# Sigmoid attention into a token and channel mixer: the first loads by other queues, weights in full-width rows, and batch 0's second channel product moved into the 64x64 runs of batch 2

## The chip, the cores and the metric

One core of one Trainium2 chip. The number is device time in microseconds (us) of one execution, the median of three runs. The engines named here are PE (matmuls; PEld is its weight load), DVE (VectorE), ACT (ScalarE), POOL (GpSimd, which here issues the loads that cast fp32 to fp16) and SP (which issues transposing DMAs and stores). Each has its own list of instructions, in the order in which the kernel issues them, and waits for the others through semaphores.

## The reference

For 8 batches, 12 heads, 448 positions and head width 64:

```python
scores = scale * np.matmul(q, k.transpose(0, 1, 3, 2)) - np.log(S)
attn = 1.0 / (1.0 + np.exp(-scores))
out = np.matmul(attn, v)
...
x = attn_out.transpose(0, 2, 1, 3).reshape(B, S, H * D)      # 8 x 448 x 768
xt = x.transpose(0, 2, 1)
h = np.maximum(xt @ w_tok1, 0.0) @ w_tok2                    # 448 -> 256 -> 448
u = x + h.transpose(0, 2, 1)
h2 = np.maximum(u @ w_ch1, 0.0) @ w_ch2                      # 768 -> 1536 -> 768
return u + h2
```

## The kernel before, in words

**Units.** The 12 heads of a batch are taken as three units of four heads: unit u holds heads 2u and 2u+1 in partitions 0 to 63 and heads 6+2u and 7+2u in partitions 64 to 127. There are 24 cycles, c = 3b + u; c5 is batch 1, unit 2, and c6, c7, c8 are batch 2. The program is written in one order by hand (a manual schedule), and each engine keeps that order.

**What a cycle holds.** `qk` (line 173) makes seven score blocks, four 64x64 matmuls each, and ACT turns each into `att` by one sigmoid. `av` (198) multiplies by v, for the unit before, and DVE casts the result from two PSUM banks into `xT` (217), then copies its last 64 columns (221). `xtrans_dma` (231) has SP transpose `xT` into `xn`. `tok_tail` and `tok1` (257, 275) are the first token product, `ytrans` (302) the second, whose sum with `xT` DVE writes to `ut` (314). A batch's three units done, `ch1` (332) makes the first channel product (12 blocks of six 128x128 matmuls, DVE's relu at 350 into `h2`), and `ch2`, `ch2_pair`, `ch2_last` (397, 443, 476) the second, which is stored from tile `outs`.

**Two forms of the second channel product.** `ch2` makes a group (128 rows, half the 768 columns) with twelve 128x128 matmuls. `ch2_pair` makes both halves at once: eight of the twelve row blocks as `quads` (354), four 64x64 matmuls each, which stand between the 64x64 matmuls of `qk` and `av`, and the other four as 128x128 matmuls in `rest`. The tensor u is added either by DVE, from `un` (a transposing DMA of `ut`, `utrans`, 319), or, for batch 0, by PE: three matmuls with the identity (416).

**Order of the cycles.** Batch 0 and c3 to c5 are written out (662 to 795). c6 to c8 are a loop of their own (798 to 847) in which `pending` deals out pieces: batch 0's `ch2` and `ch2_last` in c6 and c7, batch 1's `ch1` in c8. c5 holds the first two `ch2` groups of batch 0. From c9 (`ONE_RUN`) each cycle is the same: two score blocks, the first turn of `ch2_pair` of batch b-2, a block, `av`, two blocks, the second turn, a block, `tok_tail`, the last block, `tok1`, `rest`, `ytrans`; the third cycle of a batch also holds `ch2_last` and the next batch's 12 `ch1` blocks.

**PSUM.** Four banks (m0 to m3) are dealt in turn, in the opening by the string `OPENING_BANKS`; two tiles of two banks hold scores. From c9 on the pair uses m2 and m3, and `av`, `tok_tail` and `ytrans` use m0 and m1.

**Transposed q and k.** From batch 2, unit 1 on they come by DMA: DVE regroups a unit (`relayout`, 114, into `rel`), SP transposes (`dma_transpose`, 132, into `tr`). `by_unit` (147) lists the eight pieces for the last two units of batch 2, `through_dma` (138) those for a whole batch; the list `copies` is popped between PE's pieces. POOL holds back the loads of the batch after by a small copy that reads the end of `tr` (`gated_loads`, 723, line 725; and 793): the gate runs when that transpose has landed. `raw` has one buffer each for k and q, so batch 3's k and q can be loaded only when batch 2's have been regrouped.

**The loads.** All of v, most of q and k, and the weights go by POOL's queue in the order in which they stand (531 to 600, then 783). Each such load holds one of eight semaphores and waits for the one eight before it. `c1` and `c2` come in two column halves each. The first unit's q comes as fp32 by the ACT and SP queues (525) into `first_q`, cast by DVE and ACT (639, 640).

Of the kernel before, what the change touches and what calls it, by code (L numbers as in the profile page):

```python
# [9 lines left out]
FP16 = mybir.dt.float16  # L10
# [13 lines left out]
OPENING_BANKS = "20130130130130213021302130213021313021213021302130202130123102302132132032"  # L24
# [3 lines left out]
def kernel(  # L28
# [41 lines left out]
    first_q = pc.tile([128, 2, NJ, E], FP32, name="first_q")  # L70
# [326 lines left out]
    def ch2(b, t, half, n0=0, n1=NCB):  # L397
# [6 lines left out]
        for cb in range(n0, n1):  # L404
            nc.tensor.matmul(  # L405
                out=ps[:, 0:DH],
                lhsT=h2[b][:, cb, 128 * t : 128 * t + 128],
                rhs=c2[:, cb, cols],
                start=(cb == 0),
                stop=(cb == NCB - 1 and b in un),  # L410
            )
        if n1 < NCB:
            return
        if b not in un:
            for n in range(NU):
                nc.tensor.matmul(
                    out=ps[:, 128 * n : 128 * n + 128],
                    lhsT=uts[b % 2][:, NU * half + n, 128 * t : 128 * t + 128],
                    rhs=ident[:, :],
                    start=False,  # L420
                    stop=(n == NU - 1),
                )
        ch2_out(b, t, half, ps)

# [18 lines left out]
    def ch2_pair(b, t):  # L443
# [17 lines left out]
        def rest():  # L461
            for p in range(2):
                for n in range(n_quads, NCB):
# [5 lines left out]
                        stop=(n == NCB - 1),  # L469
                    )  # L470
                ch2_out(b, t, p, ps[p])
# [52 lines left out]

    for g, queue in enumerate((nc.scalar, nc.sync)):
        queue.dma_start(
            out=first_q[64 * g : 64 * g + 64].rearrange("p hi j e -> p hi (j e)"),
            in_=q[0, 6 * g : 6 * g + 2].rearrange("h (p j) e -> p h (j e)", j=NJ),
        )

    def load_first_k(j0, j1):
        for g in range(2):
            nc.gpsimd.dma_start(
                out=raw_tile(0, "k")[64 * g : 64 * g + 64, 0, :, j0:j1, :].rearrange(
                    "p hi j e -> p hi (j e)"
                ),
                in_=k[0, 6 * g : 6 * g + 2].rearrange("h (p j) e -> p h (j e)", j=NJ)[
                    :, :, j0 * E : j1 * E
                ],
            )  # L540

    load_first_k(0, 2)
# [7 lines left out]
    load_first_k(2, NJ)  # L550
# [21 lines left out]
    def load_c1(half):  # L572
        cols = slice(CC // 2 * half, CC // 2 * half + CC // 2)
        nc.gpsimd.dma_start(
            out=c1[:, :, cols],
            in_=moe_w_ch1.rearrange("(db d) c -> d db c", db=NDB)[:, :, cols],
        )

    def load_c2(half):
        cols = slice(DH * half, DH * half + DH)  # L580
        nc.gpsimd.dma_start(
            out=c2[:, :, cols],
            in_=moe_w_ch2.rearrange("(cb c) d -> c cb d", cb=NCB)[:, :, cols],
        )
# [3 lines left out]
    load_c1(0)  # L588
# [3 lines left out]
    load_c1(1)  # L592
# [4 lines left out]
    load(2, "k", k, 1, NU)  # L597
    load(2, "q", q, 1, NU)
    load_c2(1)
    load(2, "v", v, 0, 1)  # L600

# [22 lines left out]
    def keep_warm(n):  # L624
# [12 lines left out]
    keep_warm(16)  # L637

    nc.vector.tensor_copy(out=raw_tile(0, "q")[:, 0, :, 0:4, :], in_=first_q[:, :, 0:4, :])
    nc.scalar.activation(  # L640
        out=raw_tile(0, "q")[:, 0, :, 4:NJ, :], in_=first_q[:, :, 4:NJ, :], func=COPYF
    )
    pe_transpose(0, "q", 0, 0, 4)
    pe_transpose(0, "q", 0, 4, NJ, on_scalar=True)
    pe_transpose(0, "k", 0, 0, 2)
    keep_warm(3)
# [12 lines left out]
    def tok(u):  # L659
# [6 lines left out]
            [tp(0, 0, "k", 2), lambda: keep_warm(3)],  # L666
# [44 lines left out]
    ch1(0, 0, 0, 4)  # L711
    qk(1, 0, 4)
    qk(1, 0, 5)
    ch1(0, 1, 0, 4)
# [21 lines left out]
    ONE_RUN = 3 * NU  # L736
    LATER = 0

    by_half = sorted(((t, half) for t in range(3) for half in range(2)), key=lambda g: g[1])
    for c, cb in ((N_FIRST, 3), (N_FIRST + 1, 8)):  # L740
# [31 lines left out]
        if u == 2:  # L772
            copies = by_unit(2, 1)
        whole(cb + 2)
        if c - 1 not in ON_DMA:
            xtrans(*before)
        for t in ("k", "q"):
            pe_transpose(ahead[0], t, ahead[1])
        whole(cb + 3)
        if c == N_FIRST:  # L780
            tok1(*before)
# [3 lines left out]
        else:  # L785
            for w, f in pieces_ch2(0, by_half[:2]):
                f()
                if copies:
                    copies.pop(0)()
            while copies:  # L790
                copies.pop(0)()

            nc.gpsimd.tensor_copy(out=gate[:, :], in_=tr[2, "q"][:, 1, NJ - 1, 126:128])
            load(2, "v", v, 1, NU)
            gated_loads(b)

    pending, copies = [], []
    for c in range(2 * NU, ONE_RUN):
        b, u = divmod(c, NU)
        before, ahead = divmod(c - 1, NU), divmod(c - 2, NU)  # L800


        if c in (2 * NU, 2 * NU + 2):
            first = c
            if c == 2 * NU:
                pending, shares = [*pieces_ch2(0, by_half[2:]), *pieces_last(0)], [15, 15]
            else:
                pending, shares = list(pieces_ch1(1)), [30]
            total = sum(w for w, f in pending)
            spent = 0  # L810

        def work(share):
            goal = 3 * sum(shares[: c - first]) + share * shares[c - first]
            done = 0
# [146 lines left out]
```

## Time and profile before

| | |
|---|---|
| median of 3 runs | 360.21 us (360.18 to 361.25) |
| the profiled execution | 360.48 us |
| its span, first to last instruction | 358.7 us |
| PE busy | 351.7 us, 4099 matmuls |
| DVE, ACT, POOL busy | 184.7, 169.5, 56.3 us |
| DMA, mean over the span | 145 GB/s, 52.11 MB |
| first sigmoid of ACT starts at | 8.54 us |
| start of c5, c6, c7, c8, c9 (first `qk` matmul) | 50.66, 63.74, 73.81, 84.31, 102.95 us |

Times inside the profile are us from the span's start. A line of the timeline gives start, duration, engine, source line, operation, output and inputs, count, and in brackets how long the engine had been idle before and what released it. In the list of DMA issues the last number is the time from issue to landing. A matmul's duration is longer than its distance to the next one (matmuls overlap in the array), so PE's time is read from starts.

### The profile page before, as it was taken

The numbers are of one execution on the slowest core, as the hardware profiler recorded it, in microseconds if no ns is written. First come the engines' busy times: TensorE is split into PE (matmuls) and PEld (weight loads), VectorE is DVE, ScalarE is ACT, GpSimd is POOL, SyncE is SP. The second block draws the span as 40 slices with busy tenths as digits, with TensorE's granted clock in tenths as the row PEclk, the third lists the DMA queues.
The fourth block names the chain that finished last, engine by engine and source line by source line (L and its number), as shares of the span: only waits on it lengthen the run. The fifth ranks groups of instructions, "written<-read, shape, count | busy, mean of one in ns | idle before, by whom it ended". The sixth has DMA issues, their size and how long they took to land.

```text
span 358.7 us, 9225 instructions
## 1 busy us (share of the span) xinstructions
PE 351.7 (98%) x4099; PEld 204.3 (57%) x4099; DVE 184.7 (51%) x343; ACT 169.5 (47%) x215; POOL 56.3 (16%) x98
## 2 busy tenths in 40 slices
PE   7999999999999999999999999999999999999995
PEld 4555565555456655666556655666456655555553
DVE  2376558247455555454645655455553445516521
ACT  3996844675458810787038820777028830010000
POOL 8974330220120004000040004000010000000000
PEclk9999999999999999999999999999999999999999
DMA  7999999999998797959989597949963680047014
GB/s 122 175 176 198 205 204 196 164 203 234 186 176 153 115 199 133 206 96 195 186 125 185 121 202 128 207 94 149 227 88 75 104 155 0 13 106 141 14 46 110
DMA packets 104375, 52.11 MB, mean 145 GB/s; under 512 B 76432, under 2 KB 101264, under 8 KB 104336
## 3 DMA queue, kind: packets, MB, share of 16 engines
q1 hardware_dynamic: 78944, 29.70, 46.0%
q0 software_dynamic: 25168, 21.50, 39.0%
q8 instruction: 32, 0.52, 0.6%
q10 hardware_dynamic: 224, 0.33, 0.4%
q14 instruction: 7, 0.06, 0.0%
HBM read 43.45 MB, written 11.01 MB: 152 GB/s over the span
## 4 chain that ended last, share of the span: by engine, by line
PE 92%; ACT 4%; DMA 1%; DVE 1%; issue 0%; DVEq 0%; ACTq 0%
PE c L339 30%; PE c L362 12%; PE c L405 10%; PE qk L181 10%; PE xa L208 8%; PE tk L286 6%; PE c L464 5%; PE yt L307 5%; PE c L488 5%; ACT att L188 4%; DMA first_q<-in_q_dram 1%; PE tp_k L161 1%; PE tp_q L161 1%; PE tk L267 1%; PE heat L626 0%; DVE ut L314 0%
## 5 line engine op out<-in xcount | busy, mean ns | idle before, releaser
L188 ACT ACTIVATE att<-qk,att_bias 128x896 f16<-128x896 f32 x168 | 154.7, 1016 | 114.3 <-PE qk L181 114.2
L339 PE MATMUL c<-ut,c 128*128 128x448 f16 x552 | 108.2, 353 | 0.0
L339 PEld LDWEIGHTS <-c 128*128 128x128 f16 x552 | 52.5, 98 | 52.3 <-issue 3.5
L350 DVE TENSOR_SCALAR h<-c 128x448 f16<-128x448 f32 x96 | 59.5, 624 | 43.6 <-PE c L339 42.0
L181 PE MATMUL qk<-tr_q,tr_k 64*64 64x448 f16 x672 | 57.9, 359 | 0.2
L428 DVE TENSOR_TENSOR o<-un,c 128x384 f32<-128x384 f16 x42 | 23.3, 554 | 49.7 <-PE c L464 28.1
L217 DVE CAST xT<-xa 128x448 f16<-128x448 f32 x48 | 27.7, 620 | 40.3 <-PE xa L208 40.3
L362 PE MATMUL c<-c,h 64*64 64x384 f16 x960 | 46.6, 323 | 0.0
L208 PE MATMUL xa<-att,raw_v 64*64 64x448 f16 x672 | 39.6, 349 | 0.0
L405 PE MATMUL c<-c,h 128*128 128x384 f16 x216 | 37.5, 326 | 0.0
L362 PEld LDWEIGHTS <-h 64*64 64x64 f16 x960 | 28.1, 107 | 11.8
L181 PEld LDWEIGHTS <-tr_k 64*64 64x64 f16 x672 | 21.2, 105 | 20.1 <-issue 12.3
L300 ACT ACTIVATE h<-tk 128x256 f16<-128x256 f32 x42 | 14.4, 417 | 33.4 <-PE tk L286 33.4
L405 PEld LDWEIGHTS <-h 128*128 128x128 f16 x216 | 20.5, 98 | 14.4 <-issue 1.4
L314 DVE TENSOR_TENSOR ut<-xT,yt 128x448 f16<-128x448 f16 x48 | 27.4, 614 | 2.6 <-PE yt L307 2.5
L725 POOL COPY gate<-tr_q 128x2 f16<-128x2 f16 x6 | 1.1, 184 | 170.4 <-DMA tr_q<-rel_q 170.4
L208 PEld LDWEIGHTS <-raw_v 64*64 64x64 f16 x672 | 20.4, 107 | 11.0 <-issue 0.7
L464 PE MATMUL c<-c,h 128*128 128x384 f16 x120 | 22.0, 326 | 0.0
L307 PE MATMUL yt<-w,h 128*128 128x448 f16 x96 | 21.9, 353 | 0.0
L286 PE MATMUL tk<-xn,w 128*128 128x256 f16 (+1 forms) x156 | 21.8, 274 | 0.1
L286 PEld LDWEIGHTS <-w 128*128 128x128 f16 (+1 forms) x156 | 13.4, 98 | 7.4 <-issue 5.2
L488 PE MATMUL c<-c,h 128*64 128x384 f16 x192 | 17.3, 328 | 0.0
(58 smaller groups left out, 195.0 us busy)
## 6 DMA issues: line engine op xcount, KB each, us to landing
out_dram<-o SPq DMA_DIRECT2D x48, 192.0 KB, 3.1
c<-in_moe_w_ch_dram POOLq DMA_DIRECT2D x4, 1152.0 KB, 15.3
raw_k<-in_k_dram POOLq DMA_DIRECT2D x10, 336.0 KB, 7.2
raw_q<-in_q_dram POOLq DMA_DIRECT2D x10, 336.0 KB, 10.5
raw_v<-in_v_dram POOLq DMA_DIRECT2D x10, 336.0 KB, 5.5
out_dram<-o SPq DMA_DIRECT2D x15, 96.0 KB, 2.3
raw_q<-in_q_dram POOLq DMA_DIRECT2D x12, 112.0 KB, 5.7
raw_k<-in_k_dram POOLq DMA_DIRECT2D x12, 112.0 KB, 5.7
```

Of the source, the lines that this page charges most:

```text
L181: nc.tensor.matmul(out=ps[64 * g : 64 * g + 64, hi, 0:S], lhsT=tr[b, "k"][64 * hi : 64 * hi + 64, u, j, 64 * g : 64 * g + 64], rhs=tr[b, " ...
L188: nc.scalar.activation(out=att[b, u][:, :, j, :], in_=ps[:, :, 0:S], func=SIGMOID, bias=bias_t[:, :], scale=att_scale,)
L208: nc.tensor.matmul(out=ps[g][64 * hi : 64 * hi + 64, 0:S], lhsT=raw[b, "v"][64 * g : 64 * g + 64, u, hi, j, :], rhs=att[b, u][64 * g : 64 ...
L217: nc.vector.tensor_copy(out=xTs[b % 2][:, u, g, 0:S], in_=ps[g][:, 0:S])
L286: nc.tensor.matmul(out=ps[tcb], lhsT=w1[rows, t, cols], rhs=xn[b][rows, u, :, t, :], start=(t == 0 and not with_scores), stop=(t == (2 if ...
L307: nc.tensor.matmul(out=ps[:, 0:S], lhsT=h1[b][:, tcb, g, u, :], rhs=w2[:, tcb, :, :], start=(tcb == 0), stop=(tcb == 1),)
L339: nc.tensor.matmul(out=ps[:, 0:S], lhsT=c1[:, BY_UNIT[d], 128 * cb : 128 * cb + 128], rhs=uts[b % 2][:, BY_UNIT[d], 0:S], start=(d == 0), ...
L350: nc.vector.tensor_scalar(out=h2[b][:, cb, :], in0=ps[:, 0:S], scalar1=0.0, scalar2=None, op0=MAX)
L362: nc.tensor.matmul(out=ps[p][m : m + 64, 0:n], lhsT=lhsT(p, part, m), rhs=rhs(p, part), start=(first and turn == 0), stop=(last and turn = ...
L405: nc.tensor.matmul(out=ps[:, 0:DH], lhsT=h2[b][:, cb, 128 * t : 128 * t + 128], rhs=c2[:, cb, cols], start=(cb == 0), stop=(cb == NCB - 1 ...
L464: nc.tensor.matmul(out=ps[p][:, 0:DH], lhsT=h2[b][:, n, 128 * t : 128 * t + 128], rhs=c2[:, n, DH * p : DH * p + DH], start=False, stop=(n ...
L488: nc.tensor.matmul(out=ps[g], lhsT=h2[b][:, n, 384:448], rhs=c2[:, n, DH * g : DH * g + DH], start=(n == 0), stop=(n == NCB - 1 and not ad ...
```

## The change

Five edits:

1. The first two blocks of k for batch 0, unit 0 come as fp32 by the ACT and SP queues (`first_k`, 64 KB each); DVE casts them and ACT copies their transposes. The unit's q comes by POOL's queue, first in it, with the cast in the DMA, and is transposed in two halves by partitions, 14 transposes of 64x64 each, each half copied by DVE.
2. `c1` is loaded in three parts by unit (row blocks u and u+3, all 1536 columns), one after the other; `c2` in two halves by rows, all 768 columns. The loads of k and q for batch 2, units 1 and 2 are split, and `c2`'s second half goes between them.
3. Batch 0's first two `ch1` blocks are made in two parts (`ch1(0, cb, 0, 2)`, then `2, 4`).
4. `ONE_RUN` is 6 instead of 9: c6, c7 and c8 take the form of the later cycles, with batch 0's second channel product in them as `ch2_pair`, the sum with u made on PE (`add_u`). c5 keeps no `ch2` group.
5. The relayouts and transposes for batch 2, unit 2 move from c5 to c6, behind `rest`, and with them the gates on them; those for batch 3 move from c7 and c8 to the end of c7 and to c8.

```diff
-    load_first_k(0, 2)
+    for g, queue in enumerate((nc.scalar, nc.sync)):
+        queue.dma_start(
+            out=first_k[64 * g : 64 * g + 64], in_=first_rows[g][:, :, 0 : 2 * E]
+        )
+    load(0, "q", q, 0, 1)
...
-    load_c1(0)
+    for u in range(NU):
+        load_c1(u)
     load(1, "v", v, 0, 1)
...
     load_c2(0)
-    load(2, "k", k, 1, NU)
-    load(2, "q", q, 1, NU)
+    load(2, "k", k, 1, 2)
+    load(2, "q", q, 1, 2)
     load_c2(1)
+    load(2, "k", k, 2, NU)
+    load(2, "q", q, 2, NU)
     load(2, "v", v, 0, 1)
...
-    keep_warm(16)
...
-    pe_transpose(0, "q", 0, 0, 4)
-    pe_transpose(0, "q", 0, 4, NJ, on_scalar=True)
-    pe_transpose(0, "k", 0, 0, 2)
-    keep_warm(3)
+    keep_warm(15)
+    nc.vector.tensor_copy(
+        out=raw_tile(0, "k")[:, 0, :, 0:2, :],
+        in_=first_k.rearrange("p hi (j e) -> p hi j e", j=2),
+    )
+    pe_transpose(0, "k", 0, 0, 2, on_scalar=True)
+    for g in range(2):
+        part = slice(64 * g, 64 * g + 64)
+        ps = bank([128, NJ, 64], FP16, f"tq_{g}")
...
+        nc.vector.tensor_copy(out=tr_tile(0, "q")[:, 0, :, part], in_=ps[:, :, :])
+    keep_warm(4)
...
-    ONE_RUN = 3 * NU
-    LATER = 0
+    ONE_RUN = 2 * NU
+    LATER = 3
...
         else:
-            for w, f in pieces_ch2(0, by_half[:2]):
...
-            nc.gpsimd.tensor_copy(out=gate[:, :], in_=tr[2, "q"][:, 1, NJ - 1, 126:128])
-            load(2, "v", v, 1, NU)
-            gated_loads(b)
+            copies = by_unit(2, 1)
+            whole(cb + 2)
+            whole(cb + 3)
...
     for c in range(ONE_RUN, N_CYCLES):
...
         qk(b, u, 2)
-        if copies:
+        if copies and u > 0:
             copies.pop(0)()
             copies.pop(0)()
...
         tok1(*ahead, with_scores=True)
         rest()
+        if c == ONE_RUN:
+            while copies:
+                copies.pop(0)()
+            nc.gpsimd.tensor_copy(out=gate[:, :], in_=tr[2, "q"][:, 1, NJ - 1, 126:128])
+            load(2, "v", v, 1, NU)
+            gated_loads(b - 1)
         if u == 1 and copies:
             copies.pop(0)()
             copies.pop(0)()
         if u == 0 and LATER < b + 1 < B or u == 1 and b + 1 == LATER:
             copies = through_dma(b + 1, 0)
         if u == 2:
             at_bank[0] = Y + 1
             for w, f in pieces_last(b - 2):
                 f()
+                if len(copies) > 2:
+                    copies.pop(0)()
```

## The prediction

> **What bounds the kernel now.** I read the page's first two parts, then PE's share in stretches cut at the starts of c5 to c11, then what DVE, POOL and SP wait for there, and the landings.
>
> ```profile
> PE 351.7 (98%) x4099; PEld 204.3 (57%) x4099; DVE 184.7 (51%) x343; ACT 169.5 (47%) x215; POOL 56.3 (16%) x98
> ...
> DMA  7999999999998797959989597949963680047014
> ```
>
> PE is the bound on the average, but through the first 12 slices (to 108 us) the DMA engines are above 90% busy too. There the order of landings can end PE's work.
>
> ```profile
> 50.66:63.74 13.08, 12.99 (x175) 8.03 (x175) 8.45 (x16) 6.39 (x7) 0.54 (x1) 1.00 1.31 192
> 63.74:73.81 10.07, 10.07 (x108) 5.58 (x107) 3.29 (x7) 7.16 (x9) 4.04 (x8) 1.00 1.31 169
> 73.81:84.31 10.50, 10.50 (x125) 6.00 (x125) 5.74 (x12) 7.16 (x9) 0.21 (x1) 1.00 1.22 187
> 84.31:102.95 18.64, 18.64 (x145) 9.36 (x144) 11.79 (x22) 7.16 (x9) 4.15 (x7) 1.00 1.13 209
> 102.95:111.25 8.30, 8.30 (x145) 5.32 (x144) 3.59 (x8) 6.94 (x9) 0.00 (x0) 1.00 1.32 206
> 119.55:143.81 24.26, 24.26 (x239) 13.48 (x239) 14.15 (x26) 6.94 (x9) 4.13 (x7) 1.00 0.94 157
> ```
>
> The second number of a row is the stretch's length, the third PE's busy time: no gap in c6 to c11. c9 (8.30) and c11 (24.26) are the form that c6 to c8 will take.
>
> ```profile
> 67.72 0.18 POOL L793 COPY gate<-tr_q 128x2 f16<-128x2 f16 x1 [14.46 <-DMA tr_q<-rel_q]
> ...
> 70.86 0.18 POOL L725 COPY gate<-tr_q 128x2 f16<-128x2 f16 x1 [1.65 <-DMA tr_q<-rel_q]
> 71.39 1.31 POOL L109 DMA_DIRECT2D raw_k<-in_k_dram x2 [0.35 <-PE qk L181]
> ...
> 79.00 0.62 DVE L120 COPY rel_k<-raw_k 128x896 f16<-128x896 f16 x1 [1.24 <-DMA raw_k<-in_k_dram]
> ...
> xn<-xT SPq DMA_TRANSPOSE x1, 9.9
> w<-in_moe_w_tok_dram POOLq DMA_DIRECT2D x1, 32.0 KB, 12.9
> tr_q<-rel_q SPq DMA_TRANSPOSE x1, 4.8
> raw_k<-in_k_dram POOLq DMA_DIRECT2D x1, 336.0 KB, 6.9
> ```
>
> A chain: tr_q of batch 2, unit 2 (issued 65.97, +4.8) opens the gate at 70.86; batch 3's k is issued at 71.39 and 72.0, its second half lands at 78.9 (+6.9); DVE, 1.24 us idle, regroups it at 79.0. DVE already waits there. The xn of c4's unit, issued at 55.56 amid the loads, lands at 65.5 (+9.9), w1's last rows (issued 52.73, +12.9) at 65.6; c6 needs both at 68.38.
>
> **The parts.**
>
> *PE, c5 to c8.* c5 loses two `ch2` groups: its last `ch1` block starts at 58.27 and PE is through at 59.41, so c6 starts at 59.5 instead of 63.74. c6 and c7 cost 8.30 plus six matmuls with the identity; three of them took 0.16 (61.36 to the next group at 61.53), so 8.63 each. c8 costs 24.26 + 0.33 + 0.17 (the last rows' own six) = 24.76. Without waits c9 would start at 59.5 + 8.63 + 8.63 + 24.76 = 101.5 instead of 102.95: **-1.4**. The products are the same; what goes is the change between 128x128 and 64x64 matmuls, some 0.1 us each way (a last `ytrans` matmul to the first score block 0.28, between two `ytrans` matmuls 0.19).
>
> *Head.* Before, fp32 q lands at 5.46 (issued 0.74, +4.7), cast 0.43, 14 transposes, copies; PE then runs three heat matmuls, and the first scores start at 7.89. After, 112 KB halves of q by POOL start at 1.24 and 1.85; the like loads of the next unit took 3.6 to 3.9, so they land near 4.9 and 5.6, and half a's transposes hide before half b lands. Half b's end 0.7 later (14 took 0.7), at 6.35; beside DVE's copy (0.4) four heat matmuls, 0.2 each at this point, end at 7.15: scores **0.75 earlier**. k's part is done before q lands (64 KB in the place of 224). Bounds: half b at 4.95 (an 80 KB load of the head took 3.1) or 6.25 (the first k load, 4.4): 1.4 earlier to 0.1.
>
> *c1.* POOL's order now puts all 2304 KB of `c1` ahead of v, q, k of batch 1. From 26.1 (k's landing before it) to 40.9 (the second c1 half's) 2976 KB landed: 201 KB/us. The third part would land at 26.1 + 11.5 = 37.6, or 37.3 with longer rows (below); PE needs it for the fifth row block, at 37.66 before, at 36.9 with the head. So 0.35 of the head is left there (bounds 0 to all of it). v, q and k behind it land by 38.7 to 41.3 and are first needed at 40.1 (v) and 45 (k).
>
> *c2.* c6's pair reads rows of the second half, at 60.6; it lands behind 448 KB instead of 896, near 60. No wait (bounds 0 to 0.9).
>
> *c6's wait.* `tok_tail` is due 5.08 after c6's start (108.03 - 102.95): 64.6, or 64.25 with what is left of the head. It needs xn and w1's last rows, and the same bytes stand before them. Rows twice as long: 1152 KB took 5.6 us as c1 (1536-byte rows) and 5.75 as c2 (768); at 0.15 for each MB the four loads gain 0.6. So 65.0: **+0.4**, and the head is used up, whatever it was. Bounds: 64.2 (no wait) to 65.6 (as before).
>
> *Relayouts.* Unit 1's now stand behind c5's transposes on PE: tr_q is issued near 61.3 (61.06 before) and lands at +6.6, 67.9, before c7 reads it. For unit 2 of batch 2 they move from 60.15 to behind c6's `rest`: two DVE copies, two SP transposes, now past the xn and the two stores of c6, with the gate, v's rest and batch 3's k and q behind. Two copies before `ytrans`' sums delay c7's `av`: +0.2. Then: c6's `tok_tail` 65.0, c7 at 65.0 + 3.55 + 0.2 = 68.75 (3.22 from `tok_tail` to the next cycle in c9, and 0.33). DVE ends `rest`'s copies at 68.4, the relayouts at 69.0 and 69.55. SP: two stores 68.4 to 70.0 (1.55 before), tr_k 1.3, tr_q issued 71.3, landing +4.8: 76.1. PE needs it at 77.4: hidden by 1.3. But the gate opens at 76.1 instead of 70.86, k is issued at 76.6 (+0.53).
>
> *Who waits.* c8 starts at 68.75 + 8.63 = 77.4. After its third score block DVE has two relayouts of batch 3's k; behind them stand the casts of `av`, and behind these `tok_tail`, which writes the same banks (m0, m1). Its due time is 82.5. Issue to the second half's landing was 7.5 with 448 KB of v ahead, which is now in by 74. Below it: 672 KB at 200 KB/us, 3.4, and 2.7 for what an 80 KB load took over its own 0.4: 6.1. Nearest is the same load's 7.5; with v gone I take 7.0: 83.6. Relayouts 1.14, casts 1.16: 85.9. **+3.4**. Bounds: transposes 3.1 (the quickest xn) to 6.6 (tr_q of unit 1), loads 6.1 to 7.5: 0.8 to 5.7.
>
> *Else.* q of batch 3 lands some 12.7 behind the gate (83.6 - 70.86 before), near 89, when DVE reaches it; from c9 on the program is the same.
>
> **Sum.** -1.4 + 0.4 + 0.2 + 3.4 = +2.6 on c9's start. The profiled execution took 360.48 (span 358.7, 1.8 around it): 363.1. It lies 0.27 over the median of the runs shown, so the forecast is **362.8**.
>
> **Rivals.**
> - *Batch 3's k is there in time* (faster). If it lands by 80.2, the last term goes: 3.4 sooner than worked out. The lower bounds of transposes and load give 2.6 of that; the two stores ahead of the transposes (1.55), if these don't hold them up, the rest. For it: the DMA engines have less to do at 70 to 76 than before, as v and unit 1's transposes are through. Against: DVE waited 1.24 behind a gate that opened 5 us earlier. The time is 360.2 - 1.4 + 0.4 + 0.2 = 359.4; where xn and w1 are sooner as well, c6's wait goes and 0.35 of the head stays: 358.7.
> - *Half the wait.* Transposes and load both near their lower bounds: 0.8 to 1.9 in c8 instead of 3.4, 360.2 to 361.3.
> - *The stall also costs clock.* In the head PE stood from 4.66 to 6.04; the 14 transposes behind it took 0.96 and the first two score blocks 0.96, against 0.58 and 0.57 later, for some 3 us. A like stretch at about half pace behind c8's stall would add 1.5: 364.3. The granted clock reads 1.00 in the head as well, so it would not show there. Against it: what was slow in the head was not yet warm when it stopped.
>
> The Trainium skill (TensorE: Matmul & The Clock Gate, Part 1) says that a gap of over some 3.4 us sends PE's clock back to half for about as long. By that rule a stall of 3.4 is just at the edge, and the time would be that of this rival; the head's rows agree with a slow start, and no gap of such length behind the head is in the trace.
>
> - *The head and the wider rows do nothing.* Scores no earlier, rows no quicker: c6's wait is 1.0 instead of 0.4, 363.4, within the forecast's own range.
>
> **Numbers.** A wait of 1.9 to 4.6 in c8 (361.3 to 364.0): 0.54. With the clock, or later landings still: 0.09. Half the wait: 0.19. In time: 0.18, of which 0.15 with c6's wait gone too (under 359.1). What a measurement can tell from no change is about 0.3%, 1.1 us: slower 0.63, same 0.22, faster 0.15. The range goes from the rival in time, 358.7, to the landings' upper bounds, 360.2 - 1.4 + 0.4 + 0.2 + 5.7 = 365.1; the forecast's own is 361.3 to 364.0.
>
> **What would show it.** First scores at 7.0 to 7.4. PE idle at c1's third part near 37, and before c6's `tok_tail` until about 65, released by xn or w1. c6's and c7's lengths 9.2 and 8.6. The gate on unit 2 at 75 to 77, DVE's first relayout of batch 3 with an idle of 3 to 5 us released by raw_k, and PE idle of 2 to 4.6 before `tok_tail` in c8, released by DVE's cast. I am wrong if that relayout finds k landed, or if `tok_tail` goes ahead of it.

## The result and the profile after

| | before | after |
|---|---|---|
| median (lowest to highest) of 6 runs | 360.39 us (360.18 to 361.25) | 378.75 us (373.55 to 381.07) |
| ratio, 95% interval | | 1.046 (1.042 to 1.050) |
| the profiled execution, its span | 360.48, 358.7 us | 378.72, 377.0 us |
| start of c0, c3, c4 | 7.89, 27.67, 36.58 | 6.15, 25.84, 38.39 |
| start of c5, c6, c7, c8, c9 | 50.66, 63.74, 73.81, 84.31, 102.95 | 52.75, 61.49, 70.57, 80.99, 121.18 |

The change is slower by 4.6%, with the sign that was forecast and seven times the size. (Two of the six runs of after were in a slower state, and the ratios here and below leave such runs out, so that this one is lower than the quotient of the medians.) From c9 on both programs keep the same distance; c9 starts 18.23 later.

The stretches that the prediction showed, cut at the starts of c5 to c9 and at c11, from after (stretch, length, then busy time of PE, PEld, DVE, ACT, POOL, then granted clock, DMA share, GB/s):

```profile
52.75:61.49 8.74, 8.65 (x147) 5.35 (x146) 6.02 (x12) 6.39 (x7) 2.91 (x5) 1.00 1.19 207
61.49:70.57 9.08, 8.82 (x149) 5.51 (x148) 3.28 (x8) 7.05 (x9) 0.00 (x0) 1.00 1.31 150
70.57:80.99 10.42, 8.90 (x149) 6.18 (x149) 5.55 (x11) 6.99 (x9) 1.44 (x3) 1.00 1.05 148
80.99:121.18 40.19, 27.62 (x250) 15.78 (x249) 14.25 (x26) 7.16 (x9) 6.96 (x12) 0.83 0.91 132
121.18:129.48 8.30, 8.30 (x143) 5.32 (x142) 3.59 (x8) 6.94 (x9) 0.00 (x0) 1.00 1.26 203
```

c8 holds most of the loss: 40.19 long where 24.76 was worked out without waits, PE busy 27.62 of it, and the granted clock, 1.00 elsewhere, is 0.83 on its mean. What stands around its gap, from after's timeline (start, duration, engine, line, operation; in brackets the idle time before and what ended it):

```profile
81.07 0.18 POOL L737 COPY gate<-tr_q 128x2 f16<-128x2 f16 x1 [8.73 <-DMA tr_q<-rel_q]
81.17 5.14 SPq L321 DMA_TRANSPOSE un<-ut  x1
81.61 1.33 POOL L109 DMA_DIRECT2D raw_k<-in_k_dram  x2 [0.35 <-PE qk L181]
96.97 1.15 DVE L120 COPY rel_k<-raw_k 128x896 f16<-128x896 f16 x2 [16.59 <-DMA raw_k<-in_k_dram]
98.70 0.95 PE L267 MATMUL tk<-xn,w 64*64 64x256 f16 x4 [12.45 <-DVE xT L217]
```

And after's list of DMA issues for 80 to 98 us (the last number is us from issue to landing):

```profile
raw_k<-in_k_dram POOLq DMA_DIRECT2D x2, 336.0 KB, 14.0
...
un<-ut SPq DMA_TRANSPOSE x1, 14.9
```

Read the timeline from its bottom: `tok_tail` (L267) waits 12.45 for DVE's cast (L217); the cast stands on DVE behind two relayouts (L120); these wait 16.59 for batch 3's k; k was issued at 81.61, behind a gate that opened at 81.07. This is the chain that was forecast. But k took 15.3 from its first issue to the landing of its second half (14.63 from the second issue at 82.26, by the chain of waits), not 7.0, and the line above k's shows what ran beside it: the transposing DMA of batch 1's u into `un`, issued 0.4 ahead of k, which took 14.9 itself. Before, `un` was issued at 94.59, when no load was in flight (v's followed from 97.19 on), and took 7.2; from before's timeline and its list of DMA issues:

```profile
94.59 3.73 SPq L321 DMA_TRANSPOSE un<-ut  x1
...
un<-ut SPq DMA_TRANSPOSE x1, 7.2
```

The matmuls behind the gap are slow as well. The granted clock (the number behind POOL's count) in one-us stretches of after, around a gap in c3 and then around c8's:

```profile
34.00:35.00 1.00, 0.00 (x0) 0.00 (x0) 0.00 (x0) 0.89 (x1) 0.00 (x0) 1.00 1.09 215
...
36.00:37.00 1.00, 1.00 (x4) 0.45 (x3) 0.00 (x0) 0.00 (x0) 0.15 (x1) 0.50 1.03 196
...
89.00:90.00 1.00, 0.00 (x0) 0.00 (x0) 0.00 (x0) 0.00 (x0) 0.00 (x0) 1.00 1.59 81
90.00:91.00 1.00, 0.00 (x0) 0.00 (x0) 0.00 (x0) 0.00 (x0) 0.00 (x0) 0.65 1.54 96
...
103.00:104.00 1.00, 1.00 (x5) 0.44 (x3) 0.56 (x1) 0.00 (x0) 0.00 (x0) 0.52 0.00 0
104.00:105.00 1.00, 1.00 (x14) 0.67 (x14) 0.60 (x2) 0.00 (x0) 0.00 (x0) 1.00 0.06 16
```

PE stops at 86.2; the clock falls near 90.3 and comes back at 104.0, 5.3 after PE resumed. Against the same instructions in c11, PE is 12.6 late at `tok_tail` and 15.9 late at the first `ch1` matmul: 3.3 more, of which 0.5 is the identity matmuls of `add_u`. So c8's 40.19 are 24.76 (as forecast without waits), 12.6 of wait and 2.8 behind it. In c3 a gap of 2.16 (c1's second part, which landed at 35.23) does the same.

### The profile page after: what moved, and what is told of

Read it like the earlier page. It is cut to its first block, busy times and chain, and to the rows that moved or that the text cites. A ratio compares the mean times of both kernels' runs of the same rounds, so it can differ in the third digit from the quotient of the medians.

```text
span 377.0 us, 9544 instructions
## 1 busy us (share of the span) xinstructions
PE 354.3 (94%) x4258; PEld 207.9 (55%) x4258; DVE 184.6 (49%) x343; ACT 168.6 (45%) x214; POOL 58.9 (16%) x103
## 4 chain that ended last, share of the span: by engine, by line
PE 80%; DMA 15%; POOL 3%; DVE 1%; issue 1%; DVEq 0%; POOLq 0%
PE c L339 28%; PE c L362 12%; PE qk L181 7%; PE xa L208 6%; PE c L405 6%; PE c L465 6%; PE tk L286 4%; PE yt L307 4%; PE c L491 4%; DMA raw_k<-in_k_dram 4%; DMA c<-in_moe_w_ch_dram 3%; DMA xn<-xT 2%; DMA tr_q<-rel_q 2%; DMA raw_q<-in_q_dram 1%; DMA w2s<-in_moe_w_tok_dram 1%; POOL raw_q L109 1%
## 5 line engine op out<-in xcount | busy, mean ns | idle before, releaser
L181 PE MATMUL qk<-tr_q,tr_k 64*64 64x448 f16 x672 | 59.9, 359 | 1.7 <-DMA tr_q<-rel_q 1.5
L362 PE MATMUL c<-c,h 64*64 64x384 f16 x1152 | 56.2, 322 | 0.0
L217 DVE CAST xT<-xa 128x448 f16<-128x448 f32 x48 | 27.7, 620 | 42.0 <-PE xa L208 42.0
L362 PEld LDWEIGHTS <-h 64*64 64x64 f16 x1152 | 34.5, 107 | 13.7
L181 PEld LDWEIGHTS <-tr_k 64*64 64x64 f16 x672 | 22.7, 105 | 20.5 <-issue 11.5
L465 PE MATMUL c<-c,h 128*128 128x384 f16 x144 | 28.1, 336 | 0.0
L405 PE MATMUL c<-c,h 128*128 128x384 f16 x144 | 24.2, 326 | 0.0
L307 PE MATMUL yt<-w,h 128*128 128x448 f16 x96 | 22.7, 362 | 0.0
L109 POOL DMA_DIRECT2D raw_q<-in_q_dram x28 | 18.2, 671 | 7.8 <-DMA c<-in_moe_w_ch_dram 5.4
L405 PEld LDWEIGHTS <-h 128*128 128x128 f16 x144 | 13.8, 98 | 9.6 <-issue 0.4
L465 PEld LDWEIGHTS <-h 128*128 128x128 f16 x144 | 14.4, 101 | 7.5 <-issue 0.7
## 6 DMA issues: line engine op xcount, KB each, us to landing
c<-in_moe_w_ch_dram POOLq DMA_DIRECT2D x2, 1152.0 KB, 13.3
```

Of the source, the lines that this page charges most:

```text
L181: nc.tensor.matmul(out=ps[64 * g : 64 * g + 64, hi, 0:S], lhsT=tr[b, "k"][64 * hi : 64 * hi + 64, u, j, 64 * g : 64 * g + 64], rhs=tr[b, " ...
L217: nc.vector.tensor_copy(out=xTs[b % 2][:, u, g, 0:S], in_=ps[g][:, 0:S])
L307: nc.tensor.matmul(out=ps[:, 0:S], lhsT=h1[b][:, tcb, g, u, :], rhs=w2[:, tcb, :, :], start=(tcb == 0), stop=(tcb == 1),)
L362: nc.tensor.matmul(out=ps[p][m : m + 64, 0:n], lhsT=lhsT(p, part, m), rhs=rhs(p, part), start=(first and turn == 0), stop=(last and turn = ...
L405: nc.tensor.matmul(out=ps[:, 0:DH], lhsT=h2[b][:, cb, 128 * t : 128 * t + 128], rhs=c2[:, cb, cols], start=(cb == 0), stop=(cb == NCB - 1),)
L465: nc.tensor.matmul(out=ps[p][:, 0:DH], lhsT=h2[b][:, n, 128 * t : 128 * t + 128], rhs=c2[:, n, DH * p : DH * p + DH], start=False, stop=(n ...
```

## The experiments

My theory was that batch 3's k crawls because `un`'s transposes are in flight beside it, and that DVE's order and the clock carry its lateness to PE and add to it. The rivals: the load takes that long by itself, and only the late gate matters; or c1's order, the head and the rows of the weights hold a good part of the loss. The ratios are to runs of the kernel before on the same chip. `A` is the changed kernel, to which each edit is made unless said otherwise.

### What made k late: un's transposes beside the load

**Un later** (`A` with `utrans(1)` moved to the end of c8):

```diff
-        if u == 2:
+        if u == 2 and b > 2:
             utrans(b - 1)
...
             for n, (w, f) in enumerate(pieces_ch1(b - 1)):
                 f()
+                if b == 2 and n == 10:
+                    utrans(b - 1)
```

> After, with one move: in c8 the transposes of batch 1's u into un (issued at 81.2 after, one DMA_TRANSPOSE of 24 blocks) are issued only near the end of the same cycle, between the last ch1 pieces. Theory 1 (batch 3's k load, issued at 81.6, crawls because those transposes run beside it): k's second half lands 7 to 8 after its issue instead of 14.6, near 89.5; PE's wait before tok_tail in c8 falls from 12.45 to 5 to 6, the half-pace stretch behind it goes or is shorter, c8 takes 28 to 32 instead of 40.2: about 369 (366 to 371). Theory 2 (the load is slow by itself, un has no part): second half still lands 14 to 15 after issue, c8 about 40, about 378.

Measured 371.57 (ratio 1.032, 1.029 to 1.035). The step of the chain of waits for k, first in after and then in this kernel:

```profile
82.26 14.63 DMA raw_k<-in_k_dram
```

```profile
83.24 6.54 DMA raw_k<-in_k_dram
```

Without `un` beside it the load takes 6.54, and 7.2 from its first issue, which is how the prediction counted its 7.0. The gap falls from 12.45 to 4.36, and c8 takes 32.36 (the time and c8 lie just over the forecast's 371 and 32). Theory 1 is shown. The first matmuls behind the gap still take 0.95 instead of 0.30, though: the half-pace stretch costs 3.1 here, for a gap a third as long. The DMA engines' busy tenths and GB/s over 80 to 98 us of after show the collision itself (40 slices of 0.45 us):

```profile
DMA  9998949999009999999999999999999999999999
GB/s 272 291 336 150 157 96 287 208 170 22 6 10 277 290 273 76 71 62 61 86 77 86 83 90 127 136 147 181 184 184 194 193 194 196 185 175 181 159 155 153
```

From slice 16 to 24 (87 to 91 us) the engines are over 90% busy and move 61 to 90 GB/s; with `un` out of the way they move some 200 in the same 4 us.

**Relayouts early** (in c6 the four pieces of batch 2, unit 2 are popped behind the third score block, so that the gate opens earlier):

```diff
         if copies and u > 0:
             copies.pop(0)()
             copies.pop(0)()
+        while c == ONE_RUN and copies:
+            copies.pop(0)()
```

> After, with one move: in c6 the two relayouts and transposes of batch 2, unit 2 stand behind the third score block instead of behind the pair's rest, so that the gate on them opens earlier; un's transposes stay where they are in c8. Theory 1: tr_q lands near 73 to 75 instead of 80.9, k of batch 3 is issued near 75 and lands by 82 to 84, mostly ahead of un's issue near 80; c7's wait of 1.5 goes, c8 waits 0 to 2: 362 to 365. Theory 2 (the load takes 14 to 15 from its issue whatever runs beside it): k lands near 89 to 90, c8 waits some 6 and PE slows behind it: 369 to 372.

Measured 366.54 (1.018, 1.015 to 1.021). k was issued at 72.84, and DVE's relayout at 83.79 did not wait for it: the wait for k is gone, as expected. But c8 did not get away with 0 to 2; from this kernel's timeline:

```profile
88.14 0.30 PE L267 MATMUL tk<-xn,w 64*64 64x256 f16 x4 [3.43 <-DMA xn<-xT]
```

The xn of c6's unit, issued at 75.89 beside k and q of batch 3, landed 12.2 later. So the collision had moved: now a small transposing DMA waits in the crowd. The matmul takes 0.30, but the clock fell a little later, with PE at work; the stretch from 89 to 90 us:

```profile
89.00:90.00 1.00, 1.00 (x7) 0.57 (x6) 0.00 (x0) 1.00 (x3) 0.00 (x0) 0.56 0.97 171
```

**Both moves** (the two diffs above together), and **both with c1 by halves** (the diff below, under the parts alone):

> After with both moves: the relayouts of batch 2, unit 2 early in c6 and un's transposes late in c8. With the first move alone k of batch 3 landed in time, but PE waited 3.43 in c8 for an xn that was issued at 75.89, beside the loads of k and q (issued 72.8 to 75.5), and landed at 88; un was issued behind it, at 80.60. Theory A (any transposing DMA and the loads hold each other up, and un is only the largest): without un the loads are through by 84 to 85 and xn lands at 84 to 86: the wait in c8 falls to 0 to 1.5, no half-clock stretch: 361 to 364. Theory B (xn is held by the loads alone, un had no part): xn lands at 88 again, 366 to 367.

> The last kernel and c1 by column halves as before as well. If the stalls of the change are the order of landings and nothing else, c3 takes 10.7 instead of 12.6 (c1's half was waited for 1.58 in the experiment with halves alone) and the end comes 1 to 2 sooner than with the two moves alone: 359.5 to 363. If c6 to c8 wait for the same landings as before, whatever c3 takes, it stays within 0.7 of the two moves alone.

Measured 366.29 (1.012, 1.007 to 1.018) and 366.78 (1.014, 1.009 to 1.019). Without `un` xn was waited for as long (4.01 and 4.11): theory B holds for xn, the loads of k and q alone hold it up. With c1 by halves c6 started 2.3 sooner (59.62 instead of 61.92) and then took 1.1 longer, waiting for xn; c8 took 30.66 instead of 31.33. The time stayed within 0.5 of the two moves alone, the second case of its forecast.

**q behind xn.** The same three moves, with batch 3's q gated on that xn, and the relayouts in c6 behind `av`:

```diff
         qk(b, u, 4)
+        while c == ONE_RUN and copies:
+            copies.pop(0)()
+        if c == ONE_RUN + 1:
+            nc.gpsimd.tensor_copy(out=gate[:, :], in_=xn[2][:, 0, 1, 3, 126:128])
+            load(3, "q", q, 0, NU)
...
-            gated_loads(b - 1)
+            nc.gpsimd.tensor_copy(
+                out=gate[:, :], in_=tr[2, "q"][:, NU - 1, NJ - 1, 126:128]
+            )
+            load(3, "k", k, 0, NU)
```

> The kernel with c1 by halves, early relayouts and late un, and three differences: in c6 the relayouts of batch 2, unit 2 stand behind av and its transpose instead of ahead of them; only k of batch 3 is loaded behind the gate in c6; q of batch 3 is loaded in c7 behind a gate on the xn that c8 waited 4.1 for (issued 75.25 beside k and q, landed 88). If it is the loads beside it that hold xn up, and q's half of them does most, xn lands at 80 to 83, c8 waits 0 to 0.7, no clock drop, c8 24.8 to 25.5: 360.5 to 362.5, equal to before within its own spread. If k alone holds it as long, xn lands past 85, and the wait stays over 1.5: 363 to 366.

Measured 363.35 (1.006, 1.002 to 1.011): xn as in the first case, the time as in the second. xn landed at 82.5, PE's wait before `tok_tail` fell to 0.47 (released by DVE's cast, not by xn), and the clock stayed at 1.00. c8 still took 27.24, as the last rows' copies stood behind a relayout that waited 1.9 for q.

### What k's lateness did to PE: DVE's order

**k's relayouts later** (all eight pieces of batch 3 between the last 16 pieces of c8's `ch1`; gate and `un` as in the change):

```diff
-        if copies and u > 0:
+        if copies and u > 0 and c != ONE_RUN + 2:
             copies.pop(0)()
             copies.pop(0)()
...
-                if len(copies) > 2:
+                if len(copies) > 2 and b > 2:
...
-                if copies and n % 2 == 1:
+                if copies and (n % 2 == 1 if b > 2 else n >= 8):
```

> After, with one move: the eight relayouts and transposes of batch 3's k and q, the first two of which stood ahead of av's casts on DVE in c8, are all put between the last 16 pieces of ch1 of the same cycle; gate and un stay. If the stall is DVE's order (casts behind a relayout that waits for k), PE does not wait before tok_tail, although k lands no sooner than after (near 96); c9 then may wait up to 3 for batch 3's transposed q: 363 to 368, clock drop gone. If PE needs something else that is late there as well (xn, un, v), a wait of over 3 stays in c8 and the time is over 370.

Measured 372.66 (369.60 to 376.29; 1.029, 1.022 to 1.035); the profiled execution took 369.60. k landed no sooner (DVE found it at 96.6), and yet PE did not wait before `tok_tail` at all: the 12.45 were DVE's order. From this kernel's timeline:

```profile
83.98 0.31 PE L267 MATMUL tk<-xn,w 64*64 64x256 f16 x4
...
96.58 0.62 DVE L120 COPY rel_k<-raw_k 128x896 f16<-128x896 f16 x1 [1.99 <-DMA raw_k<-in_k_dram]
```

But the time is over the forecast, for the same late landings were met further on:

```profile
102.57 1.29 PE L339 MATMUL c<-ut,c 128*128 128x448 f16 x6 [1.83 <-DVE h L350]
108.70 0.67 PE L181 MATMUL qk<-tr_q,tr_k 64*64 64x448 f16 x8 [2.50 <-DMA tr_q<-rel_q]
```

### What the gap did to the clock

**Heat in the gap**, 90 and then 128 matmuls on zeros, whose result nobody reads:

```diff
+        if c == ONE_RUN + 2:
+            hot = pp.tile([128, 2, 512], FP32, tag="qk", bufs=2, name="hot")
+            for _ in range(90):
+                nc.tensor.matmul(
+                    out=hot[:, 0, 0:256], lhsT=warm[:, 0:128], rhs=warm[:, :],
+                    start=True, stop=True,
+                )
         at_bank[0] = Y
         tok_tail(*ahead)
```

> After, with 90 matmuls of 128x256 on a tile of zeros, into a scores bank that nobody reads, on PE ahead of tok_tail in c8, so that PE works through most of the stall (about 10 of 12.45). The output is the same. If the half-pace stretch behind the stall is the granted clock that falls in a gap (1.00 until 90, 0.50 from 92 to 104 in after), it goes: matmuls behind the stall as long as elsewhere, 2.8 sooner, about 376 (375.5 to 376.5). If the pace behind the stall comes from something else (DMA, PSUM), nothing changes: about 378.7. If heat matmuls end behind the casts, tok_tail starts up to 1 later.

> After with 128 heat matmuls in c8's stall instead of 90. With 90 PE stood for 3.41 behind the last of them, and the granted clock, 1.00 until 98, fell to 0.50 and the matmuls behind the stall took as long as without heat. With 128 (12.8 at 0.1 each) they reach the casts or some tenths past them. If a gap is what lowers the clock, it stays at 1.00 now and the lag behind the stall (3.0 over the form of c11) is gone: c8 3 shorter for the same landing of k, 375 to 377. If the clock falls for another reason, 0.50 again and 378 to 381.

Measured 379.91 (1.049, 1.043 to 1.055) with 90 and 377.31 (1.046, 1.040 to 1.052) with 128. The first forecast missed, since 3.41 of gap were left behind the heat, and that was enough. The timeline behind the heat, with 90 and then with 128:

```profile
99.25 0.95 PE L267 MATMUL tk<-xn,w 64*64 64x256 f16 x4 [3.41 <-DVE xT L217]
```

```profile
101.21 0.30 PE L267 MATMUL tk<-xn,w 64*64 64x256 f16 x2 [0.62 <-DVE xT L217]
```

The granted clock just behind it, again with 90 and then with 128:

```profile
100.00:102.00 2.00, 2.00 (x13) 1.01 (x8) 0.00 (x0) 1.28 (x2) 0.00 (x0) 0.50 0.45 85
```

```profile
102.00:104.00 2.00, 2.00 (x22) 1.39 (x17) 0.16 (x1) 1.56 (x3) 0.00 (x0) 1.00 0.48 91
```

With 128 the clock stays at 1.00, the matmul takes 0.30, and the lateness grows by 1.05 behind the stall instead of 3.30: 2.25 of c8's loss in after is the clock. (k landed 2.5 later in this execution, so that c8 is as long as in after and the median is just over the forecast's 377; the rows behind the stall decide it.)

### The parts alone

**c1 by halves** (c1's loads and batch 0's first `ch1` blocks as before):

```diff
-    for u in range(NU):
-        load_c1(u)
+    load_c1(0)
     load(1, "v", v, 0, 1)
     load(1, "q", q, 2, NU)
     load(1, "k", k, 2, NU)
+    load_c1(1)
...
-    for cb in range(2):
-        ch1(0, cb, 0, 2)
+    ch1(0, 0, 0, 4)
     qk(1, 0, 4)
     qk(1, 0, 5)
-    for cb in range(2):
-        ch1(0, cb, 2, 4)
+    ch1(0, 1, 0, 4)
```

> After, with c1 in two column halves, in the queue and in batch 0's first ch1 blocks as before. If c1's full-width parts ahead of v, q and k cost c3 its extra 3.6 (12.55 instead of 8.91), c3 returns to about 8.9 and c4 starts near 34.8, 3.6 sooner than after. c8's stall depends on the gate and is expected to stay at about 12: c9 starts some 3 to 3.6 sooner, about 375. If instead the time only moves (c5 to c7 wait for w1, xn or c2 as before), c6 starts less than 1 sooner and the total stays near 378.

Measured 376.23 (1.046, 1.040 to 1.051). c3 took 10.67 instead of 12.55, c4 started at 35.92 instead of 38.39. So between these two executions the full-width parts cost 1.9 in c3, not 3.6; 1.8 over before's 8.91 stay, 1.58 of them a wait for c1's first half, which the earlier head now meets. One execution says little here, though: c3 took 8.91 to 12.90 in the seven profiled kernels with the new head and c1 in full-width parts, 9.49 to 10.94 in the eight with the new head and c1 by halves (medians 12.13 and 10.33). c9 starts 4.7 sooner, as the stall in c8 is shorter as well (9.76): k was issued 0.1 ahead of `un` here instead of 0.4 behind it, and took 11.9 instead of 14.6. The median is within the change's own spread.

**The head alone** (the kernel before with edit 1 of the change, as its diff shows it, and nothing else):

> Before, with the head alone changed (first two k blocks as fp32 by the ACT and SP queues, q by the casting queue, transposed by partition halves; one more heat matmul). Scores start at 6.15 instead of 7.89, as after. If PE alone sets the time, all 1.74 reaches the end: 358.7. If the landings set c5 to c8 (xn and w1 for c6's tok_tail at 65.5, batch 3's k for DVE at 78.9), the gain is taken back by c6: within 0.4 of before, 360.0 to 360.4.

Measured 360.97 (1.003, 1.001 to 1.005), 0.8 over before on the same chip: no gain. In the profiled execution scores start at 6.57, 1.32 sooner, but c0 takes 7.27 instead of 6.44 and c3 9.56 instead of 8.91 (0.47 of it before c1's first half), and c6 starts at 63.86, 0.12 behind before. In c0 PE waits for nothing: up to some 9 us its matmuls go at a slower pace, as they did before (the first eight score matmuls take 0.96 in both, against 0.58 in after). So a part of the head's gain goes to this slow start, which differs between executions (cycle 1 starts at 12.0 to 13.9 in the fifteen profiles with the new head, at 14.33 in before), and a part to the landing of the weights `c1`.

**Parts 4 and 5 alone** (`A` with head, c1 and c2 as before; of the undone edits, c2's):

```diff
-        rows = slice(NCB // 2 * half, NCB // 2 * half + NCB // 2)
+        cols = slice(DH * half, DH * half + DH)
...
-    load(2, "k", k, 1, 2)
-    load(2, "q", q, 1, 2)
+    load(2, "k", k, 1, NU)
+    load(2, "q", q, 1, NU)
     load_c2(1)
-    load(2, "k", k, 2, NU)
-    load(2, "q", q, 2, NU)
```

> Before, with parts 4 and 5 of the change alone (the 64x64 runs from c6 on, the relayouts and gates moved); head, c1 and c2 as before. If these two carry the loss, c6 starts near 59.4, waits about 1 for xn and w1, c7 for tr_q about 1 to 1.5, and c8 stalls 10 to 13 before tok_tail, with half clock behind it: 375 to 380. If head, c1 and c2 were a part of it (their rows or their order), the stall is shorter: under 372.

Measured 372.04 (1.028, 1.021 to 1.036): less than the whole change, which I had not expected. In the profiled execution, the slowest of the four (375.44), c6 starts at 59.21 and waits at once (the timeline, with c8's gap):

```profile
65.47 2.77 PE L362 MATMUL c<-c,h 64*64 64x384 f16 x30 [5.52 <-DMA c<-in_moe_w_ch_dram]
94.88 0.95 PE L267 MATMUL tk<-xn,w 64*64 64x256 f16 x4 [4.58 <-DVE xT L217]
```

`ch2_pair` reads both column halves of c2 from its first matmul on; the rows of edit 2 are what part 4 needs, and they save this 5.52. What c6 loses here, c8 gains: k was issued at 84.04 and `un` 2.1 behind it (86.18) instead of 0.4 ahead, k's step of the chain is 8.43 instead of 14.63, and c8's gap 4.58 instead of 12.45. That is in line with theory 1, without an edit to `un`.

### Where the gain went

Four runs ask whether the shorter cycles can be had in another order.

**x by PE, w1 in a tile of its own** (on "q behind xn": `xtrans` on PE in c5 for the unit whose xn c6 waits for; w1's last rows loaded early into a tile `w1x`):

```diff
-    ON_DMA = range(N_FIRST, N_CYCLES)
+    ON_DMA = range(N_FIRST + 1, N_CYCLES)
...
             copies = by_unit(2, 1)
+            xtrans(*before)
             whole(cb + 2)
...
-            nc.gpsimd.dma_start(out=w1[64:128, 3, :], in_=tok_rows[NJ - 1])
...
+    for par in range(2):
+        nc.gpsimd.dma_start(out=w1x[64 * par : 64 * par + 64, :], in_=tok_rows[NJ - 1])
     load(2, "q", q, 0, 1)
```

> The same, and the two landings that c6 waits for are taken away: batch 1 unit 1's x is transposed by PE in c5 (eight transposes, some 0.45) instead of by DMA, and the last row block of w1 lies in a tile of its own, loaded with batch 2's first q and k. If c6's wait (1.75 with the three moves) is those two landings only and the DMA has room behind it, c6 takes 8.6 and c9 starts 1.3 sooner than in the kernel beside it: 359 to 361. If the landings behind it are the bound, c7 and c8 wait longer by what c6 gains: within 0.5 of the kernel beside it.

Measured 365.49 (1.012, 1.006 to 1.018), 2 more than the kernel beside it. c6 takes 8.63, with no wait, but c5 10.16 instead of 8.74; tr_q of unit 2 opens the gate only at 76.06 (71.85 there), and c8 waits 2.83 for k's relayouts. The gain came back as a wait behind it.

**DVE's order** (on "q behind xn": batch 3's first relayouts of k behind `av`'s casts, q's between `ch1`'s pieces), and with it **v later** (batch 2's first v behind a gate on the transposed k). The first, then what the second adds:

```diff
-        if copies and u > 0:
+        if copies and u > 0 and c != ONE_RUN + 2:
...
-        while c == ONE_RUN and copies:
+        while c == ONE_RUN and copies or c == ONE_RUN + 2 and len(copies) > 6:
             copies.pop(0)()
...
-                if len(copies) > 2:
+                if len(copies) > (4 if b == 2 else 2):
...
-                if copies and n % 2 == 1:
+                if copies and n % 2 == 1 and (b > 2 or n > 4):
```

```diff
-    load(2, "v", v, 0, 1)
...
+        if c == ONE_RUN:
+            nc.gpsimd.tensor_copy(out=gate[:, :], in_=tr[2, "k"][:, 1, NJ - 1, 126:128])
+            load(2, "v", v, 0, 1)
```

> The kernel with q of batch 3 behind xn, with DVE's order in c8 changed: the first two relayouts of batch 3's k stand behind av's casts instead of ahead of them, and q's relayouts between ch1's pieces instead of the last rows' pieces (there DVE waited 1.9 for q, and PE 1.3 behind it). If these waits are DVE's order only, c8 takes 24.8 to 25.3 instead of 27.2, no wait at c9: 360.0 to 361.5, the same as before. If the later relayouts make c9 wait for batch 3's transposed q, c8 keeps over 26: 362 to 363.5.

> The same, and the first unit of batch 2's v (224 KB, issued 53.9 ahead of w1's last rows and beside the xn that c6 waits for) is loaded in c6 behind a gate on batch 2's transposed k instead. If the waits are a question of order, xn and w1 land 0.6 to 1.2 sooner, c6 is shorter by as much and nothing behind it waits: 359.0 to 360.5, under before. If the bytes between 50 and 82 cannot be had sooner in any order, the same time comes back as a wait for tr_q at c7, for v there or for k in c8: within 0.5 of the kernel beside it, or slower.

Measured 365.27 (1.013, 1.011 to 1.015) and 366.22 (1.016, 1.014 to 1.017). c8 takes 24.77 in both, the forecast's 24.76. c9 starts at 103.25 and 103.06. Then c10, which none of my theories named, takes 13.38 and 14.24 instead of 8.30; the first's timeline:

```profile
120.06 0.32 PE L267 MATMUL tk<-xn,w 64*64 64x256 f16 x4 [3.26 <-DMA xn<-xT]
```

Its xn was issued at 108.27, beside v of batch 3 and k and q of batch 4 (issued 101.88 to 105.12), and landed 11.74 later, and the clock fell behind the gap. With v later, c6 lost its wait (8.70 instead of 10.30), but c7 took 10.14 instead of 8.63, 0.70 of it before v: c8 starts 0.2 sooner, not 1.2.

**q of batch 4 behind that xn too** (on "DVE's order"):

```diff
-        if c == ONE_RUN + 1:
-            nc.gpsimd.tensor_copy(out=gate[:, :], in_=xn[2][:, 0, 1, 3, 126:128])
-            load(3, "q", q, 0, NU)
+        if c in (ONE_RUN + 1, ONE_RUN + 3):
+            nc.gpsimd.tensor_copy(
+                out=gate[:, :], in_=xn[2][:, before[1], 1, 3, 126:128]
+            )
+            load(3 if c == ONE_RUN + 1 else 4, "q", q, 0, NU)
...
-        for t, src in (("k", k), ("q", q)):
+        for t, src in (("k", k), ("q", q))[: 1 if b == 2 else 2]:
```

> The kernel with DVE's order changed, and batch 4's q loaded in c9 behind a gate on the xn that c10 waited 3.26 for. If that wait is the same collision, xn lands within 6 of its issue, c10 takes 8.3 to 8.7 instead of 13.38, nothing is waited for from c7 on, and c9 starts at about 103.2, 0.3 behind before: 360.4 to 361.5. That would say that the order of landings explains all of the loss behind c6, and that the opening's landings (c1 in c3, xn and w1 in c6) hold back what the head and the modes gave. If k and v beside xn are enough to hold it up, or q then is late in c11, 362 to 366.

Measured 361.07 (359.93 to 364.55; 1.003, 1.0003 to 1.0057); the profiled execution took 360.25. c7 to c10 take 8.63, 24.78, 8.30, 8.30: nothing is waited for there any more, and 17.7 of the change's 18.4 are gone. c9 starts at 102.03, 0.92 sooner than in the profile before, but over all runs it does not beat the kernel before. What is left stands ahead of c7, a wait of 1.86 for xn in c6:

```profile
65.04 0.30 PE L267 MATMUL tk<-xn,w 64*64 64x256 f16 x4 [1.86 <-DMA xn<-xT]
```

and a c11 that is 0.67 longer (its xn, behind the q that was moved). No kernel of these was faster than before.

## Why the prediction was wrong

The sign was right, the chain was right, the size was not: 378.75 lies far over the upper bound of 365.1. The prediction's sum puts c9's start at 59.5 + 9.25 + 8.63 + 28.16 = 105.5; it was 121.2.

- **The step that failed is the term of +3.4**, "k is issued at 76.6 ... with v gone I take 7.0: 83.6". In c8 it measured 15.4: 12.6 of wait and 2.8 behind it. The gate opened at 81.1 instead of 76.1 (c6 started 2.0 later than I put it, tr_q took 7.8 instead of 4.8); c8 started 3.6 later itself, so that the late gate cost the term only 1.4. The size is in the load: it took 15.3 instead of 7.0, both from the first issue to the second half's landing, 8.3 more. I had priced it from the same load before, without asking what the new form puts beside it. The form of c9 issues `utrans` behind the third score block; the loop that it replaces issued it 10 us into the cycle. Part 4 thus moves a transposing DMA of 24 blocks by 13 us into k's load, and no sentence of mine counts it. With `un` put behind the load the 7.0 measures 7.2 (un later).
- **The chain of waits** held word for word: relayout waits for k, casts behind it, `tok_tail` behind these. With the relayouts put behind the casts the 12.45 were gone, with k as late as ever, which shows that DVE's order was the link.
- **The rival of the clock** was right in kind and came on top of the forecast case: 2.25 in c8, not 1.5 (the heat runs), and I gave it 0.09 with later landings. My sentence that the granted clock would not show it was wrong: it reads 0.50 there. The head's slow matmuls, at 1.00, were no sign for or against.
- **c5, c6, c7.** c5 took 8.74 (forecast 8.84). c6 took 9.08 (9.25), but its wait was 0.26, since it started 2 later. c7 took 10.42 (8.63): the transposes were "hidden by 1.3" and came 1.5 late, as tr_q took 7.8 beside v's loads (4.55 in parts 4 and 5 alone, where v had landed). Without waits c7 and c8 take 8.63 and 24.77 to 24.78 (the last runs), just as worked out from c9 and c11: the term of -1.4 for the modes was sound, and it was never paid out.
- **Head.** Scores start 1.74 sooner, not 0.75: the halves of q landed 2.8 and 3.3 after their issue, not 3.6 to 3.9, and from half b's landing to the first scores it took 0.9, not 1.5. That it would be used up by c6 was right in the head alone, but there it went in c0 and c3, and c6 waited for nothing.
- **c1.** I put the need at its third part, 0.35 of the head left. PE waited 2.16 already for the second part, the clock fell behind that gap, and c3 took 12.55: c4 started 1.8 later than before. I looked only at the last landing, and its rate was off as well: from k's landing to the third part's it took 13.3 instead of 11.5 (174 KB/us, not 201), 5.9 of it for the first part. That the longer rows would gain 0.6 by c6 is not to be seen either: w1's last rows landed at 66.55, not 65.0.
- **c2.** No wait, as forecast; the runs show why it matters (5.52 without the rows; 0.78 in q behind xn, within the bounds).
- **Else.** The landing of batch 3's q before is misread: its second half lands at 84.91, 14.05 behind the gate, not 12.7. Nothing in the sum hangs on it.

What stays open: why a transposing DMA and a load slow each other's packets (the rows are in the last section). No run changed how packets are formed.

## What to carry to other kernels

When a change puts a cycle into another form, list every DMA that the new form issues at another time, and price each load by what will be in flight beside it, not by what the same load took in its old place. Here, with the DMA engines over 90% busy, cycles that PE does faster only brought their deadlines forward, until the landings were put in a new order as well; the whole order (c1 by halves, early relayouts, `un` behind k, q behind xn twice, DVE's order) was worth 17.7 us and came out even with the kernel before. A wait of PE cost more than itself here from about 2 us on (1.96 left the clock alone, 2.14 lowered it).

## What the runs showed of the hardware

**Transposing DMAs and loads in flight together slow each other far beyond their bytes.** k's load takes 6.5 without `un` beside it (un later), `un` 7.2 (before), and an xn 3.8 to 4.3 at the median of a run's 20 in most runs. Together k took 14.6 and `un` 14.9 (after), and an xn beside loads 11.4 to 12.9 (relayouts early, both moves, DVE's order, v later). The packets themselves get slower. Below are packets, MB and the time that the packets took as a share of 16 engines' span: the transposes (q1) and the loads (q0) in after from 87 to 91 us, then the loads alone in un later from 87 to 91, then transposes alone in before from 94.4 to 96:

```profile
q1 hardware_dynamic: 459, 0.12, 85.9%
q0 software_dynamic: 230, 0.20, 67.9%
```

```profile
q0 software_dynamic: 927, 0.80, 125.3%
```

```profile
q1 hardware_dynamic: 1825, 0.46, 127.7%
```

Worked out from these rows (share times the time of 16 engines, divided by the packets), a transposing packet takes some 120 ns on the mean beside the load and 18 alone, a load's packet some 190 and 87. It seems to matter how close the two issues stand, though no run varied this distance alone: with `un` issued 0.4 to 0.5 ahead of k the second half of k took 14.6 to 16.9 (after, k's relayouts later, both heat runs), with `un` 0.1 behind k's first issue 11.9 (c1 by halves), 2.1 behind it 8.4 (parts 4 and 5 alone), and with `un` out of the way 6.5.

**The granted clock falls in shorter gaps than I had reckoned with.** Gaps of 1.58 to 1.96 us left it at 1.00 (c1 by halves in c3 and c6, the last run in c6). Gaps of 2.14 (both moves, c3), 2.16 (after, c3), 2.50 (k's relayouts later, c9), 2.83 (x by PE, c8) and longer took it to 0.50. In all the profiles no gap between 1.2 and 1.96 behind the head lowered it, and each of the 18 from 2.14 up did. The stretches at 0.50 last 3.41 (after, c3), 6.83 (un later, c8), 10.24 (c1 by halves, c8) or 13.65 (after, c8), one to four times the same length. It can fall when PE is already back at work: in "relayouts early" PE resumed at 88.14, and the clock fell past 89. The Trainium skill (TensorE: Matmul & The Clock Gate, Part 1) says that a free-running window of some 3.4 us decides, and that an idle window brings PE to half. That it falls late, by one half only, and for whole multiples of 3.41 agrees with these rows; that PE must stand idle for as long as that does not: here 2.14 was enough.
